# Product 2 of a Strassen-Winograd output by a second level of the method, in the free quarters of the banks of h

## The chip, the cores and the metric

One core of a Trainium2 chip runs the whole kernel. The metric is the time of one execution on the device in microseconds, the median of several runs.

## The reference

Eight heads of a linear attention without softmax, an RMS norm, and then a feed-forward layer with a leaky ReLU, all in fp32:

```python
kv = np.einsum('bhsd,bhse->bhde', k, v)            # batch 8, heads 8, seq 576, dim 64
out = np.einsum('bhsd,bhde->bhse', q, kv)
rms = np.sqrt(np.mean(out * out, axis=-1, keepdims=True) + 1e-06)
attn = out / rms * g_norm
x = attn.transpose(0, 2, 1, 3).reshape(4608, 512)
h = x @ w_in                                       # 512 x 2048
g = np.maximum(0.01 * h, h)
return g @ w_out                                   # 2048 x 512
```

Nearly all the arithmetic is in the two products with w_in and w_out, 4608 x 512 x 2048 each.

## The kernel before, in words

The 4608 tokens are cut into nine blocks of 512. Block 0 is done by plain matmuls (`first_block`). Blocks 1 to 8 (index `i` in the last loop) use the Winograd form of Strassen's method: a product of two matrices cut in 2 x 2 quarters takes seven products of quarters (or of sums of quarters) in place of eight. Its seven products are numbered 1 to 7 and done in the order 1, 2, 6, 5, 7, 3, 4 (`ORDER`). The products 1, 6, 7, 4 pile up in one bank of PSUM and 2, 5, 3 in another, where 2 and 5 start afresh (`FRESH`), so that each partial sum that the method needs stands in a bank at some moment and is taken from there.

The 2048 columns of w_in are cut into four chunks of 512 (`c`). A chunk of a block has two halves: h = x w_in and its leaky ReLU, which gives g (in four quarters g11, g12, g21, g22), and the chunk's share of the output, o, which is g times 512 rows of w_out and is added up over the four chunks in four tiles o11, o12, o21, o22 in SBUF.

h of blocks 2 to 8 (`product_h_two`) uses two levels of the method: 7 x 7 products of 128 x 128 by 128 columns. Step k of the outer seven does seven matmuls of 128 columns: the four with inner numbers 1, 6, 7, 4 go to the bank tagged ha (or hc), side by side in its four quarters of 128 columns, and the three with 2, 5, 3 go to hb (or hd), of which the fourth quarter stays empty. Steps 1, 6, 7 and 4 use ha and hb, steps 2, 5 and 3 use hc and hd. ScalarE copies the banks of steps 1, 6, 5 and 4 into SBUF, VectorE adds those of 2, 7 and 3 to what stands there. After step 4 VectorE forms the four quarters of g from these sums by seven additions, ScalarE applies the leaky ReLU to each, and GpSimd makes the four sums of quarters that the method needs (`sums_of`). g is held in two tiles used in turn by even and odd chunks.

o (`product_o`, one level) takes seven products of four matmuls, 128 rows deep and 256 columns wide, each group of four into one of the two banks oa and oc. Each product's bank is copied (ScalarE, for the first share of a block) or added (VectorE) into one of the four o tiles. The sums of quarters of w_out come from DRAM into two tiles (`pairs`), product by product.

The loop interleaves the two: in each of a chunk's seven slots (`t`) it gives one step of h, then the attention and other small work that lists such as `FINE_SLOTS` place, then one product of o. o runs two slots behind (`LAG`): the first product of a chunk's o stands in slot 2 of the next chunk, the sixth in slot 0 and the seventh in slot 1 of the chunk after. In slot 6 VectorE is also given the first two of the additions for g, and the other five follow the slot's product of o. In slots 20, 21 and 22 of a block (chunk 2 slot 6, chunk 3 slots 0 and 1) VectorE makes the sums of x for the next block, and in slots 24 and 25 and after the block GpSimd makes the second-level sums of x. In the last block the products of o are held back in slots 22 and 25 (`HELD`). Matmuls, DMA and most of VectorE's work are pinned to program order; where an instruction needs a tile that another engine reads or writes, it waits on that engine's semaphore.

The lines of the profile: L118 is the helper that issues every matmul, L610 every addition on VectorE and GpSimd, L781 the leaky ReLU, L845 ScalarE's copies of h's banks, L879 its copies of o's, L646 the loads of the sums of w_out, L708 the loads of w_in's sums. `w_all<-h_ha` and `pairs<-h_hb` are the evictions of h's banks (`qa` and `qc` in the code), and `o<-o_a` those of o's.

Of the kernel before, what the change touches and what calls it, by code (L numbers as in the profile page):

```python
# [9 lines left out]
F32 = mybir.dt.float32  # L10
# [13 lines left out]
def kernel(  # L24
# [584 lines left out]
    def add(eng, out_, a, b_, minus=False, pinned=False):  # L609
        ins = eng.tensor_tensor(out_, a, b_, op=ALU.subtract if minus else ALU.add)  # L610
        if pinned or steady and eng is nc.vector:
            pin(ins)
# [45 lines left out]


    GROUPS = (1, 6, 7, 4), (2, 5, 3)  # L660
    AT = {j: n for n, j in enumerate((5, 6, 7, 3, 1, 2, 4))}
    ORDER = (1, 2, 6, 5, 7, 3, 4)
    FRESH = (1, 2, 5)
# [96 lines left out]

        return sides, quarters, sums(), inner

    def strassen(tags, left, right, done):


        banks = {}
        for i in ORDER:
            b = tags[0 if i in (1, 6, 7, 4) else 1]
            if i in FRESH:
                banks[b] = ps_m.tile([P, 2, N2], F32, tag=b, name=f"{b[0]}_{b[1]}")  # L770
            bank = banks[b]
            for part in range(2):
                for r in range(2):
                    matmul(bank[:, part, :], lhsT=left(i, part, r), rhs=right(i, part, r),
                           start=i in FRESH and part == 0 and r == 0, stop=(r == 1),
                           skip_group_check=True)
            done(i, bank.rearrange("p u (v n) -> p (u v) n", v=2))
            yield
# [45 lines left out]
                            lambda i, part, r: x_sides[i][:, r, :], done)  # L824
        sums_of(c, to)

    def product_h_two(i, c, quarters, to):

        n0 = 7 * ((i - 2) * NC + c)

        into = {1: (0, True), 2: (0, False), 6: (1, True), 5: (3, True), 7: (3, False),
                3: (1, False), 4: (2, True)}
        banks = {}
        for t, k in enumerate(ORDER):
            for js, tags, q in zip(GROUPS, (("ha", "hc"), ("hb", "hd")), (qa, qc)):
                tag = tags[0 if k in (1, 6, 7, 4) else 1]
                if k in FRESH:
                    banks[tag] = ps_m.tile([P, len(js), P], F32, tag=tag, name=f"h_{tag}")
                for n, j in enumerate(js):
                    matmul(banks[tag][:, n, :], lhsT=w_place(n0 + t)[:, AT[j], :],  # L840
                           rhs=quarters[k][j], start=k in FRESH and n == 0, stop=True,
                           skip_group_check=True)
                at, fresh = into[k]
                if fresh:
                    nc.scalar.copy(q[:, at], banks[tag])  # L845
                else:
                    add(nc.vector, q[:, at], banks[tag], q[:, at])
            read(n0 + t + 1 + RING)
            yield
        g11, g21, g22, g12 = g_of(c)  # L850
        add(nc.vector, g21, qa[:, :, 0, :], qa[:, :, 1, :])
        add(nc.vector, g11, qa[:, :, 0, :], qc[:, :, 0, :])
        yield
        add(nc.vector, g22, g21, qa[:, :, 2, :])
        add(nc.vector, g12, g22, qa[:, :, 3, :])
        yield
        add(nc.vector, g22, g22, qc[:, :, 1, :])
# [6 lines left out]
    def product_o(n, g_sides, os, finish):  # L864
# [124 lines left out]
    HELD = (22, 25)  # L989
    o_queue, waited = collections.deque(), 0  # L990

    def go_o():
        while o_queue:
            if next(o_queue[0], o_queue) is not o_queue:
                return True
            o_queue.popleft()

    for i in range(1, NB):
        one = i == 1
        steady = not one  # L1000
        late, a_steps = a_steps, attention(i + 1, fine=not one) if i + 1 < B else iter(())
        os = {}
        for c in range(NC):
            g_sides = {}
            h_steps = product_h(c, h_sides, x_sides, g_sides) if one else \
                product_h_two(i, c, quarters, g_sides)
            for t in range(7):
                slot = 7 * c + t
                go(h_steps, 1)
                if not one:  # L1010

                    if t == 6:
                        go(h_steps, 1)
                    if slot in LATE_SLOTS:
                        go(late, 1)
                    for _ in range(FINE_SLOTS.get(slot, 0)):
                        go(a_steps, 1)
                    if i + 1 < NB:
                        if slot == 20:
                            x_sides, new_quarters, sums, inner = sides_x(i + 1)  # L1020
                        if slot in (20, 21, 22):
                            go(sums, 2 if slot == 20 else 1)
                        if slot == 24:
                            inner(0)
                        elif slot == 25:
                            inner(1)
                    load_some()
                if slot in HELD and i == NB - 1:
                    pass
                elif waited == LAG:  # L1030
                    go_o()
                elif o_queue:
                    waited += 1
                if one:

                    if t == 1:
                        combine(c, 2)
                    if t == 3 and c < NC - 1:
                        h_sides, more_h = sides_w1(c + 1)
                        combine(c + 1, 0)  # L1040
                    if t == 5 and c < NC - 1:
                        more_h()
                        combine(c + 1, 1)
                    if slot == 4:
                        go(late, 1)
                    if slot in A_SLOTS:
                        go(a_steps, 1)
                    load_some()
                    if slot == 24:
                        go(a_steps)  # L1050
                        x_sides, new_quarters, sums, inner = sides_x(i + 1)
                        go(sums)
                    elif slot == 25:
                        inner(0)
# [11 lines left out]
            o_queue.append(product_o((i - 1) * NC + c, g_sides, os, store(i)))  # L1066
    while go_o():
        pass

# [29 lines left out]
```

## Time and profile before

The time is 927.6 us (three runs, 926.85 to 929.41). The profile is of one execution with a span of 925.5 us.

| engine | busy, us | share of the span | instructions |
|---|---|---|---|
| TensorE, matmuls (PE) | 915.1 | 99% | 6856 |
| TensorE, weight loads (PEld) | 776.5 | 84% | 6856 |
| VectorE (DVE) | 615.5 | 67% | 998 |
| ScalarE (ACT) | 328.7 | 36% | 651 |
| GpSimd (POOL) | 317.6 | 34% | 318 |

The engines run side by side, each in its own order, so that the shares don't add up to one. An fp32 matmul stands in the records as two passes with a weight load each. A line of the timeline gives the start in microseconds from the span's start, the duration, the engine, the line of the code, the operation, output and input tiles (buffer numbers left out), sizes and count; at the end, in brackets, how long the engine was idle before it and what released it. Lines that follow each other with the same tiles are merged.

### The profile page before, as it was taken

The page shows a single profiled execution, that of the slowest core. Times are in us where ns is not written, and L with a number is a line of the kernel's source. Part 1 is how long each engine was busy: PE and PEld are TensorE (multiplying, and loading weights), DVE is VectorE, ACT ScalarE, POOL GpSimd, SP SyncE. Part 2 cuts the span into 40 slices and gives each one's busy share as a digit, 9 for nine tenths or more (in the row PEclk, how much of TensorE's full clock was granted, in tenths as well). Part 3 has the DMA queues.
Part 4 walks back from the last instruction along what each step waited for, and adds up shares of the span by engine and source line. Part 5 has one row for each costly group of instructions (what it writes and reads, how often), then busy time and mean ns, then how long its engine had stood idle before and what let it go on. Part 6 is the DMA issues. An engine that isn't in the chain of part 4 may idle for free.

```text
span 925.5 us, 17566 instructions
## 1 busy us (share of the span) xinstructions
PE 915.1 (99%) x6856; PEld 776.5 (84%) x6856; DVE 615.5 (67%) x998; ACT 328.7 (36%) x651; POOL 317.6 (34%) x318
## 2 busy tenths in 40 slices
PE   8999999999999999999999999999999999999998
PEld 5544447888998999899999999999988999999996
DVE  4866995587456876597757875687558744654454
ACT  4544532242135233532343423342333333223330
POOL 2000354967622542236211711272225322532222
PEclk9999999999999999999999999999999999999999
DMA  9999936895598678856995599668755676667632
GB/s 270 223 234 217 238 114 193 276 301 165 150 348 266 185 208 297 274 174 189 280 297 181 173 282 276 219 183 229 252 174 175 197 220 186 185 196 220 187 121 91
DMA packets 90066, 200.03 MB, mean 216 GB/s; under 512 B 9856, under 2 KB 42112, under 8 KB 89984
## 3 DMA queue, kind: packets, MB, share of 16 engines
q1 hardware_dynamic: 79392, 186.85, 68.9%
q10 hardware_dynamic: 10144, 10.88, 3.4%
q8 instruction: 55, 0.90, 0.4%
q0 software_dynamic: 448, 1.18, 0.3%
q14 instruction: 27, 0.22, 0.1%
HBM read 172.39 MB, written 26.48 MB: 215 GB/s over the span
## 4 chain that ended last, share of the span: by engine, by line
PE 95%; DMA 2%; DVE 2%; issue 0%; ACT 0%; POOL 0%; SPq 0%; ACTq 0%; DVEq 0%; POOLq 0%
PE o_a L118 21%; PE o_c L118 21%; PE h_ha L118 11%; PE h_hb L118 8%; PE h_hc L118 8%; PE h_hd L118 6%; PE o_acc L118 6%; PE h_ps L118 6%; PE o_ps L118 2%; PE kv_ps L118 2%; PE h_a L118 1%; PE h_b L118 1%; DMA pairs<-in_v_dram 1%; PE h_c L118 1%; PE h_d L118 1%; DMA pairs<-in_moe_w_in_dram 1%
## 5 line engine op out<-in xcount | busy, mean ns | idle before, releaser
L610 POOL TENSOR_TENSOR gs<-g 128x512 f32<-128x512 f32 x64 | 80.8, 1282 | 442.3 <-ACT g L781 442.3
L610 DVE TENSOR_TENSOR o<-o_c,o 128x512 f32<-128x512 f32 x104 | 71.6, 688 | 117.8 <-PE o_c L118 117.6
L781 ACT ACTIVATE g<-g 128x512 f32<-128x512 f32 x124 | 78.2, 631 | 123.4 <-DVE g L610 123.4
L845 ACT COPY w_all<-h_ha 128x512 f32<-128x512 f32 x84 | 48.7, 580 | 186.6 <-PE h_ha L118 186.6
L610 DVE TENSOR_TENSOR o<-o_a,o 128x512 f32<-128x512 f32 x88 | 60.4, 687 | 63.4 <-PE o_a L118 63.3
L118 PE MATMUL o_c<-pairs,gs 128*128 128x256 f32 x384 | 91.3, 381 | 0.0
L118 PE MATMUL o_a<-pairs,gs 128*128 128x256 f32 x384 | 90.8, 379 | 0.0
L118 PEld LDWEIGHTS o_c<-pairs,gs 128*128 128x128 f32 x384 | 69.8, 190 | 9.3 <-issue 1.4
L118 PEld LDWEIGHTS o_a<-pairs,gs 128*128 128x128 f32 x384 | 69.8, 190 | 7.8
L118 PE MATMUL o_c<-w,g 128*128 128x256 f32 x256 | 61.6, 383 | 0.0
L118 PE MATMUL o_a<-w,g 128*128 128x256 f32 x256 | 61.5, 383 | 0.0
L118 PEld LDWEIGHTS h_ha<-stage,w_all 128*128 128x128 f32 x448 | 58.7, 192 | 2.8
L118 PE MATMUL h_ha<-stage,w_all 128*128 128x128 f32 x448 | 59.0, 275 | 0.0
L118 PE MATMUL h_ps<-xT,w_all 128*128 128x512 f32 (+1 forms) x136 | 57.9, 570 | 0.2 <-DVE w_all L255 0.2
L118 PE MATMUL o_acc<-w,g 128*128 128x512 f32 x128 | 57.8, 595 | 0.0
L610 DVE TENSOR_TENSOR g<-g,pairs 128x512 f32<-128x512 f32 x84 | 55.6, 689 | 1.9
L118 PEld LDWEIGHTS o_a<-w,g 128*128 128x128 f32 x256 | 46.4, 190 | 11.0 <-ACT pairs L845 3.1
L610 POOL TENSOR_TENSOR pairs<-w_all 128x512 f32<-128x512 f32 x8 | 11.5, 1438 | 123.5 <-DMA stage<-in_moe_w_in_dram 95.1
L118 PEld LDWEIGHTS o_c<-w,g 128*128 128x128 f32 x256 | 46.4, 190 | 5.8
L118 PEld LDWEIGHTS h_ps<-xT,w_all 128*128 128x128 f32 x136 | 25.5, 190 | 29.2 <-issue 26.5
L118 PEld LDWEIGHTS o_acc<-w,g 128*128 128x128 f32 x128 | 24.0, 190 | 29.8 <-issue 29.4
L610 DVE TENSOR_TENSOR w_all<-h_hc,w_all 128x512 f32<-128x512 f32 x56 | 38.4, 686 | 15.6 <-PE h_hc L118 15.4
(196 smaller groups left out, 2028.0 us busy)
## 6 DMA issues: line engine op xcount, KB each, us to landing
w_all<-w SPq DMA_DIRECT2D x196, 448.0 KB, 4.3
pairs<-w SPq DMA_DIRECT2D x56, 512.0 KB, 4.5
out_dram<-o ACTq DMA_DIRECT2D x36, 256.0 KB, 4.5
v_in<-in_v_dram SPq DMA_DIRECT2D x29, 288.0 KB, 5.7
k_in<-in_k_dram SPq DMA_DIRECT2D x28, 288.0 KB, 6.3
q_in<-in_q_dram SPq DMA_DIRECT2D x56, 144.0 KB, 6.6
q_in<-in_q_dram SPq DMA_DIRECT2D x56, 140.0 KB, 6.6
w<-stage SPq DMA_DIRECT2D x12, 512.0 KB, 4.6
```

The source lines that it names most:

```text
L118: pin(nc.tensor.matmul(*args, **kw))
L610: ins = eng.tensor_tensor(out_, a, b_, op=ALU.subtract if minus else ALU.add)
L781: nc.scalar.activation(t, t if src is None else src, func=AF.Prelu, alpha=SLOPE)
L845: nc.scalar.copy(q[:, at], banks[tag])
```

## The change

For 28 chunks (from the third of block 1 to the second of block 8), product 2 of o, which is g12 times the lower left quarter of w_out's chunk, is no longer done as four matmuls of 256 columns in o's own order. It is done by a second level of the method: seven products of 128 x 128 by 128 columns. Each of the seven has its place in the step of h with the same number, two chunks later, and goes into the empty fourth quarter of hb or hd, whose pattern of fresh starts and piling up is the one that it needs. VectorE adds that quarter into one quarter of o11 after each step (`Second.done`).

For it GpSimd makes four differences and sums of g12's quarters in each chunk (`inner_g`, into free room of `pairs`), and once for each of the four chunks of w_out those of its quarter (`inner_w2`, over a part of w_out that is no longer used). o's order becomes 1, 5, 6, 3, 7, nothing, 4, the slot of "nothing" being slot 0 of a chunk; the tiles of o are taken in another order, since o11 is now finished last; and the load of the first pair of w_out's sums follows product 6. The purpose is fewer columns on TensorE: seven matmuls of 128 columns in place of four of 256.

```diff
+    INTO = {1: (0, 0), 2: (0, 0), 6: (0, 1), 3: (0, 1), 7: (1, 1), 5: (1, 1), 4: (1, 0)}
...
-    def strassen(tags, left, right, done):
+    def strassen(tags, left, right, done, order=ORDER):
...
-        for i in ORDER:
+        for i in order:
+
+            if i is None:
+                yield
+                continue
...
+    gi = view(pairs, 12 * P, 4, P)
...
+    def inner_g(c, half):
+
+        g = g_of(c)[3]
+        a11, a21, a12, a22 = (g[:, n, :] for n in range(4))
+        s1, s2, s3, s4 = (gi[:, n, :] for n in range(4))
+        if half == 0:
+            add(nc.gpsimd, s1, a21, a22)
+            add(nc.gpsimd, s2, s1, a11, True)
+        else:
+            add(nc.gpsimd, s3, a11, a21, True)
+            add(nc.gpsimd, s4, a12, s2, True)
+
+    class Second:
...
+        def product(self, k, bank):
+            matmul(bank, lhsT=self.left[k], rhs=self.right[k], start=False, stop=True,
+                   skip_group_check=True)
+
+        def done(self, k, bank):
+            v, s = INTO[k]
+            to = self.o[:, v, s * P:s * P + P]
+            add(nc.vector, to, bank, to)
+            if self.n % NC == NC - 1 and k == ORDER[-1]:
+                self.finish("11", self.o)
+
-    def product_h_two(i, c, quarters, to):
+    def product_h_two(i, c, quarters, to, second):
...
-                    banks[tag] = ps_m.tile([P, len(js), P], F32, tag=tag, name=f"h_{tag}")
+                    banks[tag] = ps_m.tile([P, 4, P], F32, tag=tag, name=f"h_{tag}")
                 for n, j in enumerate(js):
                     matmul(banks[tag][:, n, :], lhsT=w_place(n0 + t)[:, AT[j], :],
                            rhs=quarters[k][j], start=k in FRESH and n == 0, stop=True,
                            skip_group_check=True)
+                if len(js) < 4 and second:
+                    second.product(k, banks[tag][:, 3, :])
                 at, fresh = into[k]
+                bank = banks[tag][:, :len(js), :]
                 if fresh:
-                    nc.scalar.copy(q[:, at], banks[tag])
+                    nc.scalar.copy(q[:, at], bank)
                 else:
-                    add(nc.vector, q[:, at], banks[tag], q[:, at])
+                    add(nc.vector, q[:, at], bank, q[:, at])
+                if len(js) < 4 and second:
+                    second.done(k, banks[tag][:, 3, :])
...
-            for key in ("11", "12", "21", "22"):
+
+            for key in ("12", "22", "11", "21"):
...
-            if i == 5:
+            if i == (6 if second else 5):
                 sums(0)
...
-                            lambda i, part, r: w_sides[i][:, r, :], done)
+                            lambda i, part, r: w_sides[i][:, r, :], done,
+                           (1, 5, 6, 3, 7, None, 4) if second else ORDER)
...
+                now = (i - 1) * NC + c
+                if now >= NC - 1 and now - 1 in seconds:
+                    for half in range(2):
+                        if t == (6 if one or half else 4):
+                            inner_g((now - 1) % NC, half)
+                    if t == 5 and now <= 2 * NC - 2:
+                        inner_w2((now - 1) % NC)
...
+            by_two = NC - 2 <= n < NC * (NB - 1) - 2
+            if by_two:
+                seconds[n] = (os, store(i))
```

More of the change, by code (lines that the diff above doesn't have):

```diff
@@ L825, in product_h, with inner_w2, __init__ @@
         sums_of(c, to)
-    def product_h_two(i, c, quarters, to):
+    gi = view(pairs, 12 * P, 4, P)
+    def inner_w2(c):
+        y = w2_sb[1][c]
+        t1, t2, t3, t4 = (w2_sb[0][c][:, u, N2 + s * P:N2 + s * P + P]
+                          for u in range(2) for s in range(2))
+        y11, y12, y21, y22 = (y[:, u, s * P:s * P + P] for u in range(2) for s in range(2))
+        add(nc.gpsimd, t1, y12, y11, True)
+        add(nc.gpsimd, t2, y22, t1, True)
+        add(nc.gpsimd, t3, y22, y12, True)
+        add(nc.gpsimd, t4, y21, t2, True)
+    def inner_g(c, half):
[9 more added lines that the diff above has]
+    class Second:
+        def __init__(self, n, o, finish):
+            self.n, self.o, self.finish = n, o, finish
+            c = n % NC
+            g, y = g_of(c)[3], w2_sb[1][c]
+            ts = [w2_sb[0][c][:, u, N2 + s * P:N2 + s * P + P]
+                  for u in range(2) for s in range(2)]
+            self.left = {1: g[:, 0, :], 2: g[:, 2, :], 4: g[:, 3, :],
+                         **{k: gi[:, at, :] for at, k in enumerate((5, 6, 7, 3))}}
+            self.right = {1: y[:, 0, :P], 2: y[:, 1, :P], 3: y[:, 1, P:N2],
+                          **{k: ts[at] for at, k in enumerate((5, 6, 7, 4))}}
+        def product(self, k, bank):
[8 more added lines that the diff above has]
+    def product_h_two(i, c, quarters, to, second):
         n0 = 7 * ((i - 2) * NC + c)
@@ L862, in product_h_two, with product_o @@
         sums_of(c, to)
-    def product_o(n, g_sides, os, finish):
+    def product_o(n, g_sides, os, finish, second):
         c = n % NC
@@ L990, with second_of @@
     o_queue, waited = collections.deque(), 0
+    seconds = {}
+    def second_of(n):
+        if n in seconds:
+            os_, finish = seconds.pop(n)
+            return Second(n, os_["11"], finish)
     def go_o():
@@ L1005 @@
             h_steps = product_h(c, h_sides, x_sides, g_sides) if one else \
-                product_h_two(i, c, quarters, g_sides)
+                product_h_two(i, c, quarters, g_sides, second_of((i - 1) * NC + c - 2))
             for t in range(7):
@@ L1065 @@
                 read((2, 4, RING, RING)[c])
-            o_queue.append(product_o((i - 1) * NC + c, g_sides, os, store(i)))
+            n = (i - 1) * NC + c
+            by_two = NC - 2 <= n < NC * (NB - 1) - 2
+            if by_two:
+                seconds[n] = (os, store(i))
+            o_queue.append(product_o(n, g_sides, os, store(i), by_two))
     while go_o():
```

## The prediction

> **What bounds the kernel now.** I read the share of busy time and the chain of waits first, then the groups by shape, then the timeline around one place: the seam between two chunks of h.
>
> ```profile
> PE 915.1 (99%) x6856; PEld 776.5 (84%) x6856; DVE 615.5 (67%) x998; ACT 328.7 (36%) x651; POOL 317.6 (34%) x318
> PE 95%; DMA 2%; DVE 2%; issue 0%; ACT 0%; POOL 0%; SPq 0%; ACTq 0%; DVEq 0%; POOLq 0%
> ```
>
> TensorE is the bound, and the chain that ends last runs through it for 95% of the span. So a microsecond less of TensorE is a microsecond less of time, as long as nobody makes TensorE wait. What it waits for are banks of PSUM, and who empties them, and when, is seen in the timeline. This is the seam of two chunks in a stretch with little else to do (lines chosen; start, duration, engine, instruction):
>
> ```profile
> 475.37 1.89 PE L118 MATMUL o_a<-pairs,gs 128*128 128x256 f32 x8
> 475.57 0.48 ACT L845 COPY pairs<-h_hb 128x384 f32<-128x384 f32 x1
> 475.57 0.69 DVE L610 TENSOR_TENSOR g<-w_all 128x512 f32<-128x512 f32 x1 [2.16 <-ACT w_all L845]
> ...
> 477.10 0.38 PE L118 MATMUL h_ha<-xT,w_all 128*128 128x128 f32 x2
> ...
> 477.30 0.69 DVE L610 TENSOR_TENSOR o<-o_a,o 128x512 f32<-128x512 f32 x1 [0.43 <-PE o_a L118]
> ...
> 479.42 2.02 DVE L610 TENSOR_TENSOR g<-g,pairs 128x512 f32<-128x512 f32 x3
> ...
> 480.39 0.38 PE L118 MATMUL h_hc<-xT,w_all 128*128 128x128 f32 x2
> ...
> 481.47 0.63 ACT L781 ACTIVATE g<-g 128x512 f32<-128x512 f32 x1 [0.42 <-DVE g L610]
> 481.95 1.89 PE L118 MATMUL o_a<-pairs,g 128*128 128x256 f32 x8
> 482.01 0.46 ACT L845 COPY pairs<-h_hb 128x384 f32<-128x384 f32 x1
> ...
> 483.68 0.50 PE L118 MATMUL h_ha<-stage,w_all 128*128 128x128 f32 x3
> ```
>
> Call 475.37, where step 4 of a chunk's h has ended, zero. TensorE then does o (to 1.73), h step 1 (to 3.29), o, h step 2, o, and h step 6 at 8.31: a product of o is always 1.73 us and a step of h 1.56, without a gap. Beside it runs a chain: VectorE makes the four g of the chunk that ended (7 adds) with o's evictions between them, ScalarE applies the leaky ReLU to each, and only behind the last ReLU does ScalarE copy the hb bank of step 1 out, 6.64 to 7.10. Step 6 writes that bank from 8.31 + 0.89 = 9.20 on. The slack is 2.1 us.
>
> The same copy in a seam where VectorE also makes sums of x (zero is 499.40), in a seam at a block's end where GpSimd is busy (zero is 523.43), and in the last seam (zero is 880.51), where one product of o is held back:
>
> ```profile
> 500.83 0.69 DVE L610 TENSOR_TENSOR w_all<-xT 128x512 f32<-128x512 f32 x1
> ...
> 506.87 0.46 ACT L845 COPY pairs<-h_hb 128x384 f32<-128x384 f32 x1
> ```
>
> ```profile
> 523.63 1.11 DVE L610 TENSOR_TENSOR g<-w_all 128x512 f32<-128x512 f32 x1 [0.87 <-ACT w_all L845]
> ...
> 530.23 0.46 ACT L845 COPY pairs<-h_hb 128x384 f32<-128x384 f32 x1
> ```
>
> ```profile
> 887.09 1.06 PE L118 MATMUL h_ha<-stage,w_all 128*128 128x128 f32 x8
> 887.14 0.46 ACT L845 COPY pairs<-h_hb 128x384 f32<-128x384 f32 x1
> ```
>
> It ends at 7.93, 7.26 and 7.09. In the last seam step 6 stands at 6.58 and needs hb at 7.47: slack 0.4.
>
> [...] The trace shows each fp32 matmul as two passes with two loads, starting every 111 ns at 128 columns and every 213 ns at 256; a quarter-size matmul therefore can't go much under 0.22 us. [...]
>
> ```profile
> L610 DVE TENSOR_TENSOR w_all<-h_hc,w_all 128x512 f32<-128x512 f32 x56 | 38.4, 686 | 15.6 <-PE h_hc L118 15.4
> L610 DVE TENSOR_TENSOR pairs<-h_hd,pairs 128x384 f32<-128x384 f32 x56 | 31.0, 553 | 0.0
> ```
>
> [...] the first add at the block's end takes 1.11 us against 0.69.
>
> **The change part by part.**
>
> *TensorE.* 28 chunks lose product 2 of o (4 matmuls, 1.73 us) and gain 7 matmuls of 128 columns. From the timeline, 8 passes of h_ha take 0.89, so two take 0.2225, and seven matmuls 1.56. Gain 0.17 a chunk, 28 x 0.17 = 4.8 us. This is all there is to win: 922.8.
>
> *Added work elsewhere.* GpSimd: 4 subtractions of 128x128 a chunk (a 128x128 one there takes 0.45 to 0.68 us in the groups by shape, so 1.8 to 2.7 us, on an engine 34% busy; their last wait is for step 3, so they are done by the seam). VectorE: seven adds of 128x128[...], for one of 0.69: 1.3 us a chunk, 37 us in all at 67% busy, hidden inside a chunk because h and o banks there come round after 5 to 6 us. The table of w2 for it is made once on GpSimd, and "11" of a block is stored two chunks later, both beside other work: nothing. The loads of the w2 sums are asked for at least three slots ahead of their use, some 10 us, and land in 4.5 us (the DMA issues): nothing.
>
> *The wait at the seam.* Here the change does three things at once. First, o's slot at step 1 is empty (the None in the order): TensorE goes from step 1 straight to step 2, and step 6 comes 1.73 us earlier, less twice 0.22 for the quarters in steps 1 and 2: hb is written at 9.20 - 1.73 + 0.44 = 7.91, its first weight load at 7.80. Second, each fresh bank hb now has two readers, ScalarE for three quarters and VectorE for the fourth[...]. In the built order VectorE's add for step 4 stands ahead of the adds for g, and its add for step 1 behind them. Third, step 6's first matmul into hb waits for that last add. Queued behind it on TensorE is everything.
>
> Quiet seam: the copy of step 4 ends at 0.68; VectorE's quarter 0.78 to 1.07 (0.1 for a hand-over between engines, as between the copy and the add at 475.57); g starts at 0.98 instead of 0.20, the second add 1.59, o's eviction 2.20 instead of 1.93 (it used to wait 0.43 for TensorE, which takes up part of the delay). From that eviction to the end of the copy of step 1 it is 7.10 - 1.93 = 5.17, so the copy ends at 7.37, the quarter at 7.76, TensorE may go at 7.8. It wants 7.80. A tie: 0 to 0.15, I take 0.05, for 14 seams 0.7 us.
>
> Seam with sums of x (one in each of six blocks): two more adds fill the gap, so the whole delay of 0.76 comes through: 7.93 + 0.76 = 8.69, quarter to 9.08, go at 9.1: wait 1.3, 6 x 1.3 = 7.8 us.
>
> Seam at a block's end (six): 7.26 + 0.5 to 0.78 (part is won back because the adds then miss some of GpSimd's work): go at 8.15 to 8.45, wait 0.35 to 0.65, I take 0.5: 3.0 us.
>
> Last seam: go at about 7.8 as in the quiet one; hb is wanted at 6.58 - 1.73 + 0.44 + 0.89 - 0.11 = 6.07: 1.7 us.
>
> Sum: 0.7 + 7.8 + 3.0 + 1.7 = 13.2 of waits, less 4.8: +8.4, **936.0 us**. Bounds: with 0 in quiet seams, 1.2 and 0.35 in the others and 1.5 in the last 10.8, so 933.6; with 0.15, 1.5, 0.8 and 1.9 17.8, so 940.6.
>
> **The rivals.** *A: no wait.* Only the 4.8 us count: 922.8. For it: TensorE has no gap anywhere in the steady part, and the skipped eviction frees VectorE at 5.99 (the o add after the adds for g). Against: that add comes after the chain, and takes nothing off it. *B: waits at the busy seams alone, and shorter* (VectorE's and ScalarE's hand-overs cost less than I put, some 0.4 us at each): 6 x 0.9 + 1.3 + 6 x 0.1 = 7.3, less 4.8: 930.1. *C: VectorE becomes the bound in stretches.* In halves of a block with attention it is busy about 80% (40.3 of the 50 us from 600 to 650, in the table of stretches), the fresh steps' quarters make it wait for ScalarE, and the backlog reaches the quiet seams: another 0.6 us in each of 14: 944.4. Against: one to two microseconds a chunk leave it below 90%.
>
> **How the numbers follow.** Forecast 0.62, A 0.12, B 0.13, C 0.13. B lies at the edge of "same" and gives it half. Faster 0.12, same 0.07, slower 0.81. The range holds the forecast with its bounds, B, and most of C, and leaves out A and the worst of C: 927 to 944.
>
> **What would show it.** Right: weight loads of h_hb at step 6 waiting for VectorE's add into o, 1 us and more once in each block, near none in quiet seams; matmuls of h_hb and h_hd into the fourth quarter at 0.22 us; VectorE's busy time up by some 35 us. Wrong: no such wait (A), waits at steps 7, 3 or 4 or at o's banks (C), or the first weight load of hb going ahead of the quarter's add.

## The result and the profile after

The changed kernel takes 940.15 us (median of four runs, 938.09 to 942.89) against 928.5 (four runs, 926.85 to 929.84) of the kernel before on the same chip. The ratio is 1.0128, with a 95% interval of 1.0096 to 1.0161: slower, and close to the 936.0 of the forecast, on the high side of it. On the base of 927.6 us, to which the ratios below are also brought, it is 939.5.

Engines and the chain of work that ended last, from the page of the kernel after (span 938.6 us):

```profile
PE 917.5 (98%) x7024; PEld 780.2 (83%) x7024; DVE 642.8 (68%) x1166; ACT 329.0 (35%) x651; POOL 374.1 (40%) x446
PE 80%; DVE 11%; ACT 3%; POOL 2%; issue 1%; DMA 1%; SPq 0%; ACTq 0%; DVEq 0%
```

TensorE's busy time didn't fall (917.5 us against 915.1), though its columns did: the ends of matmuls are modelled in these records, and a part of a short wait is counted as busy (in the seam below, eight passes of h_ha from 513.17 stand for 1.05 us, where the starts of eight take 0.89). The second line is the one to read. The chain that sets the end ran through TensorE for 95% of the span; now 14% of it is VectorE's and ScalarE's. They have not become the bound by their sums (68% and 35% busy), but in short stretches TensorE stands behind them.

The groups by shape (busy us and mean ns of one, then the idle time before them and what ended it):

```profile
L610 DVE TENSOR_TENSOR o<-h_hb,o 128x128 f32<-128x128 f32 x112 | 32.2, 287 | 83.9 <-ACT pairs L906 83.9
L118 PE MATMUL h_hb<-stage,w_all 128*128 128x128 f32 x336 | 48.0, 279 | 9.2 <-DVE o L610 9.2
L610 POOL TENSOR_TENSOR pairs<-g 128x128 f32<-128x128 f32 x56 | 25.5, 455 | 77.3 <-PE h_hb L118 62.9
L610 DVE TENSOR_TENSOR o<-h_hd,o 128x128 f32<-128x128 f32 x84 | 23.9, 284 | 39.5 <-ACT pairs L906 38.9
```

The first line holds both halves of the forecast mechanism. The new quarter add costs 287 ns, and the idle time before it was ended by ScalarE's copy of the other three quarters, all 83.9 us of it. The two engines take turns at the bank in this trace: in the seam shown below the add starts 0.03 us after the copy has ended. The second line is the price on TensorE: 9.2 us before matmuls of h_hb, ended by that add. The weight loads tell the same story in the list of waits, 8 times and at most 1.3 us: six seams with sums of x, the last seam, and one at the entry to block 2.

```profile
PEld h_hb L118 <- DVE o L610: 9.2, 8, 1.3
```

A seam with sums of x in the timeline (lines chosen); step 4 has ended, and zero is, at 506.14:

```profile
506.39 0.48 ACT L906 COPY pairs<-h_hb 128x384 f32<-128x384 f32 x1 [0.31 <-PE h_hb L118]
506.90 0.29 DVE L610 TENSOR_TENSOR o<-h_hb,o 128x128 f32<-128x128 f32 x1 [1.65 <-ACT pairs L906]
507.11 0.68 DVE L610 TENSOR_TENSOR g<-w_all 128x512 f32<-128x512 f32 x1
...
513.17 1.05 PE L118 MATMUL h_ha<-stage,w_all 128*128 128x128 f32 x8
513.80 0.63 ACT L787 ACTIVATE g<-g 128x512 f32<-128x512 f32 x1 [0.42 <-DVE g L610]
514.34 0.46 ACT L906 COPY pairs<-h_hb 128x384 f32<-128x384 f32 x1
514.83 0.29 DVE L610 TENSOR_TENSOR o<-h_hb,o 128x128 f32<-128x128 f32 x1 [1.06 <-ACT pairs L906]
515.18 0.94 PE L118 MATMUL h_hb<-stage,w_all 128*128 128x128 f32 x6 [0.95 <-DVE o L610]
```

VectorE's quarter of step 4 runs from 0.76 to 1.05, and g starts at 0.97 where it started at about 0.2. The copy of hb ends 8.66 after zero, the quarter at 8.98, TensorE restarts at 9.04. The prediction had 8.69, 9.08 and 9.1.

Where the 11 us went. From the starts of the matmuls I took, for each product of o and each step of h, what it lasted beyond its 1.73 and 1.56 us, in both traces. From the first step of block 2's h to the end, the kernel before takes 925.51 - 231.36 = 694.15 us and the kernel after 938.64 - 233.41 = 705.23, which is 11.1 more:

| where | predicted, us | in the trace, us |
|---|---|---|
| fewer columns | -4.8 | -4.8 (8 passes of h_hb take 0.89, two 0.2225) |
| six seams with sums of x | 6 x 1.3 = 7.8 | 6 x 1.22 = 7.3 |
| six seams at a block's end | 6 x 0.5 = 3.0 | 6 x 0.50 = 3.0 |
| last seam | 1.7 | 1.6 |
| fourteen quiet seams | 0.7 | 0.2 |
| entry to block 2 | 0 | 2.8 |
| banks of o, at 321, 811 and in the last block | 0 | 0.7 |
| sum | +8.4 | +10.8 |

A wait's number includes some 0.1 us by which the next matmul came late after TensorE had stood still (an example is at 259.24 below: two passes in 0.49 us in place of 0.38 to 0.39); 0.3 of the 11.1 us are not placed. The rest of the difference between the two profiled spans, 2 us, lies ahead of block 2, where the changed parts don't run (the first matmul of block 0's output stands at 36.15 against 34.11). In this profile and in two others (sums of x later, without the add of step 1) the granted clock of TensorE was 0.5 for 3.4 us from about 19 us on, and these three start latest, at 36.1 to 36.2; all the others lie between 33.5 and 35.1, kernels with the same beginning among them. So these 2 us are of the execution and not of the kernel.

The entry is the part that the prediction doesn't have. In the timeline of the kernel after, lines chosen: GpSimd (POOL), SyncE's queue (SPq), ScalarE's queue (ACTq), ScalarE and TensorE.

```profile
240.33 0.46 POOL L610 TENSOR_TENSOR pairs<-pairs,g 128x128 f32<-128x128 f32 x1
...
241.42 0.46 POOL L610 TENSOR_TENSOR pairs<-g,pairs 128x128 f32<-128x128 f32 x1
...
248.22 0.87 POOL L610 TENSOR_TENSOR w<-w 128x128 f32<-128x128 f32 x2
...
249.05 0.99 POOL L610 TENSOR_TENSOR w<-w,w 128x128 f32<-128x128 f32 x2
...
249.99 1.27 POOL L610 TENSOR_TENSOR pairs<-w,pairs 128x512 f32<-128x512 f32 x1
...
251.29 0.32 SPq L654 DMA_DIRECT2D w<-pairs  x1
...
252.18 2.15 SPq L159 DMA_DIRECT2D q_in<-in_q_dram  x4
...
258.17 0.39 ACTq L970 DMA_DIRECT2D out_dram<-o  x1
258.60 0.59 ACT L906 COPY w_all<-h_ha 128x512 f32<-128x512 f32 x1 [11.80 <-PE o_c L118]
259.24 0.49 PE L118 MATMUL h_ha<-xT,w_all 128*128 128x128 f32 x2 [0.73 <-ACT w_all L906]
```

The same sum of w_out in the kernel before:

```profile
245.33 1.29 POOL L610 TENSOR_TENSOR pairs<-w,pairs 128x512 f32<-128x512 f32 x1
```

Read from the bottom. The step 4 whose bank ha ScalarE copies at 258.60 began at 254.83, so the bank was full by about 256; ScalarE came late because its own store of o12 stood ahead, and TensorE paid 0.9 us here and 1.0 more at the next step 6. In the trace ScalarE's wait ahead of this store ends at 258.12, 0.03 us after the third of the four loads of q from 252.18 on has landed (at 258.09), and in the built program the store waits for the semaphore that an earlier load of q raises. These loads were asked for shortly behind the store of w_out's sums, which waited for GpSimd's last sum of w_out (249.99 to 251.26). GpSimd had no idle time to speak of from 230.3 to 252.6 (busy for 8.00 of the 8 us from 232 to 240, for 7.92 of those from 240 to 248); its new sums for the second level (the first four lines, 2.8 us in all) stand in that row of work. Counted from the first step of block 2's h, that last sum of w_out starts at 16.6 us; in the kernel before at 14.0 (245.33 - 231.36). A third wait, of 0.7 us near 240, is TensorE's own for GpSimd's first sums of g12.

### The profile page after: what moved, and what is told of

It is laid out like the page before. It is cut to its first block, busy times and chain, and to the rows that moved or that the text cites. A ratio compares the mean times of both kernels' runs of the same rounds, so it can differ in the third digit from the quotient of the medians.

```text
span 938.6 us, 18186 instructions
## 1 busy us (share of the span) xinstructions
PE 917.5 (98%) x7024; PEld 780.2 (83%) x7024; DVE 642.8 (68%) x1166; ACT 329.0 (35%) x651; POOL 374.1 (40%) x446
## 4 chain that ended last, share of the span: by engine, by line
PE 80%; DVE 11%; ACT 3%; POOL 2%; issue 1%; DMA 1%; SPq 0%; ACTq 0%; DVEq 0%
PE o_c L118 15%; PE o_a L118 15%; PE h_hb L118 9%; DVE g L610 8%; PE h_ha L118 8%; PE h_hd L118 6%; PE h_hc L118 6%; PE o_acc L118 6%; PE h_ps L118 6%; PE o_ps L118 2%; PE kv_ps L118 2%; DVE o L610 2%; PE h_a L118 1%; POOL stage L610 1%; ACT pairs L906 1%
## 5 line engine op out<-in xcount | busy, mean ns | idle before, releaser
L610 POOL TENSOR_TENSOR gs<-g 128x512 f32<-128x512 f32 x64 | 83.2, 1320 | 274.7 <-ACT g L787 272.6
L610 DVE TENSOR_TENSOR o<-h_hb,o 128x128 f32<-128x128 f32 x112 | 32.2, 287 | 83.9 <-ACT pairs L906 83.9
L610 DVE TENSOR_TENSOR o<-o_c,o 128x512 f32<-128x512 f32 x90 | 61.8, 686 | 32.7 <-PE o_c L118 27.3
L610 DVE TENSOR_TENSOR o<-o_a,o 128x512 f32<-128x512 f32 x74 | 50.7, 685 | 34.3 <-PE o_a L118 34.0
L118 PE MATMUL h_hb<-stage,w_all 128*128 128x128 f32 x336 | 48.0, 279 | 9.2 <-DVE o L610 9.2
L610 POOL TENSOR_TENSOR pairs<-g 128x128 f32<-128x128 f32 x56 | 25.5, 455 | 77.3 <-PE h_hb L118 62.9
L118 PEld LDWEIGHTS h_hb<-stage,w_all 128*128 128x128 f32 x336 | 41.9, 192 | 11.8 <-DVE o L610 9.2
L610 DVE TENSOR_TENSOR o<-h_hd,o 128x128 f32<-128x128 f32 x84 | 23.9, 284 | 39.5 <-ACT pairs L906 38.9
L906 ACT COPY pairs<-h_hb 128x384 f32<-128x384 f32 x84 | 39.8, 474 | 25.8 <-PE h_hb L118 25.4
```

The lines of the kernel that those rows point to most:

```text
L118: pin(nc.tensor.matmul(*args, **kw))
L906: nc.scalar.copy(q[:, at], bank)
```

## The experiments

Ratios are against the kernel before; us are those ratios times 927.6, so that runs of different chips can be read side by side.

| kernel | ratio, 95% interval | us | extra in a seam with sums of x |
|---|---|---|---|
| changed kernel | 1.0128, 1.0096 to 1.0161 | 939.5 | 1.22 |
| empty slot after product 5 (gap_mid) | 0.9974, 0.9964 to 0.9983 | 925.2 | 0 |
| empty slot after product 6 (gap_5) | 0.9987, 0.9974 to 0.9999 | 926.4 | 0 |
| new order of o alone | 1.0008, 0.9996 to 1.0019 | 928.3 | 0 |
| empty slot, no second level | 0.9544, 0.9528 to 0.9559 | 885.3 | 0.6 |
| without the adds of steps 1 and 4 | 0.9993, 0.9983 to 1.0002 | 926.9 | 0.15 |
| without the add of step 1 | 1.0064, 1.005 to 1.0078 | 933.5 | 0.9 |
| without the add of step 4 | 1.0026, 1.0016 to 1.0037 | 930.0 | 0.45 |
| last ReLUs after step 1 | 1.0059, 1.0038 to 1.0079 | 933.1 | 0.75 |
| sums of x two slots later | 1.0113, 1.0095 to 1.013 | 938.1 | 0.1 |
| store of o12 by SyncE | 1.0103, 1.0087 to 1.012 | 937.2 | 1.22 |
| entry's new sums by VectorE | 1.0152, 1.013 to 1.0174 | 941.7 | 1.22 |
| the same, empty slot after product 5 | 1.0021, 1.0008 to 1.0034 | 929.5 | 0 |

**Move the empty slot.** The theory: TensorE waits because the empty slot at step 1 brings step 6 1.73 us closer, while the chain that empties hb got longer. The rival: the two readers of the bank cost this anywhere. The empty slot goes from slot 0 of the later chunk to slot 4 of the earlier one, so that products 3 and 4 of o stand between the steps of a seam again:

```diff
-                           (1, 5, 6, 3, 7, None, 4) if second else ORDER)
+                           (1, 5, None, 6, 7, 3, 4) if second else ORDER)
```

> The changed kernel with o's order 1, 5, nothing, 6, 7, 3, 4: the empty slot moves from slot 0 to slot 4 of a chunk, away from the seam; all else stays. Theory (the empty slot at the seam brings step 6 forward by 1.73 us, before VectorE's add of step 1): step 6 wants hb at 9.5 again while the add is done at 7.8 to 9.1, so the waits of 1.2, 0.5 and 1.6 us at the seams go, the gain of 4.8 on TensorE stays, and some 2 us of waits at the entry from block 1 may stay: 925, 0.3 to 0.5% under the kernel before. Rival (the seven added VectorE operations and the second reader cost wherever they stand): 936 to 940.

It takes 0.9974 of the time before, the fastest of the versions that compute all of the output and faster than both kernels. The same copy and add in a seam with sums of x (step 6 begins at 506.77):

```profile
506.21 0.46 ACT L906 COPY pairs<-h_hb 128x384 f32<-128x384 f32 x1
506.70 0.29 DVE L610 TENSOR_TENSOR o<-h_hb,o 128x128 f32<-128x128 f32 x1 [1.06 <-ACT pairs L906]
506.77 1.05 PE L118 MATMUL h_ha<-stage,w_all 128*128 128x128 f32 x8
507.56 0.75 PEld L118 LDWEIGHTS h_hb<-stage,w_all 128*128 128x128 f32 x6
```

The chain is the same to the hundredth (the quarter again starts 1.06 us after VectorE's last work), but the weight load of hb comes 0.57 us after the quarter has ended, and has no wait. So the second reader costs nothing where a product of o covers it. Of the 4.8 us won, some 2.0 are still given back: 0.8 at the entry, 0.2 at the end, and two waits for a bank of o, of which this is the larger:

```profile
304.36 1.99 PE L118 MATMUL o_c<-pairs,gs 128*128 128x256 f32 x8 [0.39 <-DVE o L610]
```

Here product 7 follows product 6 into the same bank in the very next slot. That makes -2.8, and the ratio says -2.4.

The other place for the empty slot, between product 6 and product 7:

```diff
-                           (1, 5, 6, 3, 7, None, 4) if second else ORDER)
+                           (1, 5, 6, None, 7, 3, 4) if second else ORDER)
```

> The changed kernel with o's order 1, 5, 6, nothing, 7, 3, 4: the empty slot at slot 5. With the empty slot at slot 4 products 6 and 7 stood in neighbouring slots and in the same bank, and 7 waited 0.4 to 0.6 us for VectorE in the blocks without attention beside it; here a step and a slot lie between. Theory: those waits go, the seams stay free of waits (hb wanted at 9.5, add done by 9.1 to 9.5 in seams with sums): within 1 us of the run with the gap at slot 4 or up to 1 us less, 0.3 to 0.4% under the kernel before. Rival (VectorE is late at the seam, since step 3 and step 4 now follow each other and step 3's evictions lie right ahead of step 4's add): 2 to 4 us more.

The seams are free here too, and what is left is 0.3 at each of two banks of o and 1.7 at the entry. Its interval and that of the version above overlap (0.9974 to 0.9999 and 0.9964 to 0.9983), so it is no better.

**The order without the rest.** The kernel before with the new order of o, the new order of its tiles and the later load of w_out's sums, product 2 done in full in the slot that the change leaves empty:

```diff
-        for i in ORDER:
+        for i in order:
...
-            for key in ("11", "12", "21", "22"):
+            for key in ("12", "22", "11", "21"):
...
-            if i == 5:
+            if i == (6 if by_two else 5):
...
-                            lambda i, part, r: w_sides[i][:, r, :], done)
+                            lambda i, part, r: w_sides[i][:, r, :], done,
+                           (1, 5, 6, 3, 7, 2, 4) if by_two else ORDER)
```

> The kernel before with the changed kernel's order of o for the same 28 chunks, product 2 itself standing in the slot that is empty there (1, 5, 6, 3, 7, 2, 4), the o tiles in the changed order and the first load of w_out's sums after product 6. No second level. Theory: order, tiles and load cost nothing: 927 to 929, like the kernel before. Rival (part of the loss is o's banks, tiles or loads in the new order): 931 or more, with waits of weight loads of oa and oc.

1.0008, no measurable difference, and no new wait in its trace. Order, tiles and load cost nothing by themselves.

**The empty slot without the second level.** The same order with None for product 2. Product 2 of those 28 chunks is left out altogether, so the time shows what the empty slot does, and without any wait it would be 927.6 - 28 x 1.73 = 879.2. Of its edit against the kernel before, the line that leaves the slot empty:

```diff
-                            lambda i, part, r: w_sides[i][:, r, :], done)
+                            lambda i, part, r: w_sides[i][:, r, :], done,
+                           (1, 5, 6, 3, 7, None, 4) if by_two else ORDER)
```

> The kernel before in the changed order with the empty slot at the seam (1, 5, 6, 3, 7, nothing, 4) and product 2 left out of 28 chunks altogether, with no second level: every hb bank has one reader, ScalarE. It saves 28 x 1.73 = 48.4 us on TensorE: 879.2 without waits. Theory (the empty slot alone already makes a wait where g's chain is long): step 6 wants hb at 9.20 - 1.73 - 0.11 = 7.36, the copy ends at 7.93 in six seams with sums (wait 0.65), at 7.1 to 7.3 elsewhere (none), and 1.5 in the last seam: 884 to 885. Rival (no wait without the second reader): 879 to 880.

It gives 885.3, 6 us above that. No quarter is read by VectorE here, and still TensorE stands, now behind ScalarE's copy:

```profile
PEld h_hb L118 <- ACT pairs L848: 4.5, 7, 1.0
```

Seven times: 0.5 us (once 0.85) at each seam with sums of x, and 1.06 plus 0.35 in the last. Another 1.6 us lie at the entry to block 2, where TensorE waits for loads of w_in's sums. So the empty slot alone uses up the slack where g's chain is long. Step 6 comes 0.45 us earlier here than in the changed kernel, since steps 1 and 2 have no quarter products (2 x 0.2225); with these, but without the two adds, 0.15 us of the 0.6 is left in a seam with sums, as the next experiment shows.

**The two quarter adds at a seam.** Three kernels leave out VectorE's add of the fourth quarter into o11 after step 1, after step 4, or after both; the product on TensorE stays, only that share of o11 is never added.

```diff
-            add(nc.vector, to, bank, to)
+            if k not in (1, 4):
+                add(nc.vector, to, bank, to)
```

> The changed kernel without VectorE's adds of the quarters of steps 1 and 4 (so product 2's shares of these two steps are left out of the output); the matmuls and the empty slot stay. Theory (the wait needs both causes): the hb bank of step 1 has one reader again and g is no longer delayed by step 4's quarter, so the copy ends at 7.9 in seams with sums and at 7.1 to 7.3 in the others, against 7.8 wanted: waits of 0.2 in six seams, 1.1 in the last, none at block ends: 930 to 932. Rival (the empty slot alone): 938 to 940. Rival (the second reader alone, the slot doesn't matter): 925.

> The changed kernel without VectorE's add of the quarter of step 1 alone (its share of product 2 is left out of the output). Theory (two delays add up: step 4's add holds g back by 0.76 us, step 1's comes 0.3 to 0.4 us behind ScalarE's copy): the copy still ends at 8.66 in seams with sums, go at 8.75 against 7.8 wanted: 0.95 in six seams, 0.1 at block ends, 1.35 in the last: 934 to 936. Rival (the second reader of step 1's own bank is all of it): 928 to 930, as without both adds.

> The changed kernel without VectorE's add of the quarter of step 4 alone (its share of product 2 is left out of the output). Theory: g is no longer held back, the copy of step 1 ends at 7.9 in seams with sums, VectorE's add at 8.3, go at 8.4 against 7.8: 0.6 in six seams, none at block ends, 1.45 in the last: 932 to 933. Rival (step 4's add is all of it): 928 to 930. With the run without step 1's add, the two savings should come to 11 or 12 us together.

Without both, 926.9, some 3 us under the 930 to 932 expected, though the waits themselves are near those of the expectation: 0.15 a seam with sums, 0.96 in the last, and the entry. By the number alone the rival of the second reader alone (925) is as near; it fails on the kernel with the empty slot after product 5, where the second reader stays and costs nothing. Without step 1's add alone, 933.5, in the expected range, and TensorE's weight loads wait for ScalarE's copy in place of VectorE:

```profile
PEld h_hb L118 <- ACT pairs L907: 6.5, 8, 1.0
```

Without step 4's add alone, 930.0, below the 932 to 933 expected and at the edge of what the rival said (step 4's add is all of it: 928 to 930). What speaks against the rival are the loads, which still wait for VectorE's add of step 1, 4.5 us in all:

```profile
PEld h_hb L118 <- DVE o L610: 4.5, 8, 1.3
```

So of the 1.22 us in a seam with sums, step 4's add (0.7 us at the head of g's chain, since everything on VectorE is queued behind its wait for ScalarE) brings about 0.75, and step 1's, at the tail, about 0.35. The two savings, 5.9 and 9.5 us by the ratios, add up to 15.4, not to the 11 or 12 expected nor to the 12.5 of both together. In the traces, from the first step of block 2's h to the end, they are 4.6 and 7.2 against 11.4, which does fit; the ratio of the changed kernel, which enters the sum of the savings twice, is known to some 3 us only.

**Shorten the chain another way.** If the chain is what counts, work taken out of it elsewhere must help too. The leaky ReLU of g22 and g21 and GpSimd's sums of g are given out after step 1 of the next chunk, behind ScalarE's copy of hb:

```diff
-        for t in (g11, g12, g22, g21):
-            relu(t)
-        sums_of(c, to)
+        relu(g11)
+        relu(g12)
+
+        def rest():
+            relu(g22)
+            relu(g21)
+            sums_of(c, to)
...
+            pending.append(rest)
```

> The changed kernel, but in each seam the leaky ReLU of g22 and g21 and GpSimd's sums of g are given out after step 1 of the next chunk's h, so that ScalarE's copy of step 1's hb stands ahead of the last ReLU. Theory (the whole chain of g's additions, ReLUs, copy of hb and VectorE's quarter is what TensorE waits for): the copy still can't run before VectorE's last three additions have read the old copy, so that only the last ReLU's part of the chain falls away, some 0.4 us a seam: the seams with sums of x wait 0.8 in place of 1.2 us, the block ends 0 to 0.1 in place of 0.5, the last seam 1.2 in place of 1.6; 934 to 936 us, unless the later ReLUs delay a product of o that reads g22 or g21. Rival (the wait is one between ScalarE and VectorE on the bank alone, 0.3 to 0.4 us): no change, 940.

933.1: the theory's direction and size, a little better than it said. The copy of hb ends at 8.19 in place of 8.66, and the waits fall to 0.65, to 0 to 0.24 at the block ends, and to 0.92 in the last seam. The rival, which put the wait down to the bank alone, falls: the bank's readers are unchanged here.

**Take the sums of x out of those seams.** They go from slots 20 and 21 to slots 22 and 23:

```diff
-                        if slot == 20:
+                        if slot == 22:
...
-                        if slot in (20, 21, 22):
-                            go(sums, 2 if slot == 20 else 1)
+                        if slot in (22, 23):
+                            go(sums, 3 if slot == 22 else 1)
```

> The changed kernel with VectorE's sums of x moved from slots 20, 21 and 22 to slots 22 (three) and 23 (one), behind the seam between chunks 2 and 3. Theory (in those six seams the two sums fill the gap that swallows the delay elsewhere): their waits of 1.2 us go to near 0 as in quiet seams, 6 x 1.2 = 7.2 us less; o's first banks may wait up to 0.5 us instead: 933 to 936. Rival (the sums' place doesn't matter, the wait is 1 us in every such seam for other work of that part of the block): 938 to 940.

The seams' waits fell to 0.1 at most, as the theory said, but the time is 938.1, not the 933 to 936 expected. The saving came back two slots on, in the timeline of this kernel:

```profile
419.40 1.75 DVE L610 TENSOR_TENSOR xT<-xT 128x512 f32<-128x512 f32 x1
...
421.08 0.68 DVE L610 TENSOR_TENSOR o<-o_c,o 128x512 f32<-128x512 f32 x1
...
421.86 1.97 PE L118 MATMUL o_c<-pairs,gs 128*128 128x256 f32 x8 [0.77 <-issue]
```

VectorE's sums of x now stand ahead of its eviction of product 4 from oc, which ends at 421.76, and product 5 starts 0.1 us after it. The releaser is given as "issue", that is, the profile names none; the eviction is the one reader of that bank, and the next start follows it. Such waits of 0.6 to 1.9 us in six blocks sum to 6.9 us. So VectorE has room for these sums in neither of the two places that were tried.

**The store at the entry.** o12 of block 1 is stored by SyncE, so that ScalarE has nothing to wait for:

```diff
-            nc.scalar.dma_start(
+            (nc.sync if i == 1 and key == "12" else nc.scalar).dma_start(
```

> The changed kernel, but the store of o12 of block 1 is issued by SyncE in place of ScalarE; nothing else. Theory (at the entry to block 2 ScalarE stood still behind this store, which waited for an earlier load of q, and so copied ha of step 4 two microseconds late): TensorE's waits of 1.0 and 1.1 us between 258 and 266 us go, the one of 0.7 us for GpSimd near 240 stays; some 2 us less, 938. Rival (ScalarE was late for another cause, VectorE's or GpSimd's work at the entry): the copy of ha comes as late as before and the time stays at 940.

ScalarE's part of the theory holds: neither wait of TensorE behind the late copy of ha is there any more. But two others have come, 0.3 and 1.3 us, so that the waits of the entry come to 2.3 us in place of 2.6 (the 2.8 of the table counts the late starts after them too). The larger, with the load that it is for:

```profile
263.70 2.47 SPq L710 DMA_DIRECT2D w_all<-w  x3
...
267.06 1.13 PE L118 MATMUL h_hc<-stage,w_all 128*128 128x128 f32 x8 [1.14 <-DMA w_all<-w]
```

Counted from the first step of block 2's h, this load is asked for at 32.1 us, in the changed kernel at 31.9 (265.34 - 233.41). So it comes when it came before, and TensorE, freed of the earlier waits, is only there earlier to wait for it. In both kernels the DMA engines are busy all the time from 256 to 272: none of the 40 slices of 255 to 272 has them under 80%, and they move 357 GB/s in the mean. The ratio's interval overlaps that of the changed kernel: no gain is shown, and taking away the store's wait alone is not enough.

**The entry's new sums off GpSimd.** In the last chunk of block 1 and the first of block 2, VectorE makes the second-level sums of g12 and of w_out:

```diff
-    def inner_w2(c):
+    def inner_w2(c, eng):
...
-        add(nc.gpsimd, t1, y12, y11, True)
+        add(eng, t1, y12, y11, True)
...
+                eng = nc.vector if now <= NC else nc.gpsimd
                 if now >= NC - 1 and now - 1 in seconds:
```

and likewise `inner_g`; once in the changed kernel, and once with the empty slot after product 5.

> The changed kernel, but in the last chunk of block 1 and the first of block 2 the second-level sums of g12 and of w_out are made by VectorE, which is about half busy there, in place of GpSimd, which has no idle time there from 230 to 253 us. Theory (the entry's loss begins on GpSimd: its sums for the second level push w_out's sums back by 2.6 us against the first step of block 2; SyncE stands behind the store of these sums, asks for q 2.6 us later, and ScalarE's store of o12 waits for q): the waits of 0.7, 0.9 and 1.0 us at the entry go, q is asked for some 2 us earlier, 2 to 3 us less in all, a ratio near 1.010; the seams stay as they are. Rival (the DMA engines are full there, and the q loads land late however early they are asked for): the wait of 0.7 goes, the others stay, a ratio near 1.012.

> The order with the empty slot after product 5 (slot 4), and the entry's second-level sums by VectorE as in the kernel beside it. Theory: the seams stay free, the 0.8 us at the entry go as well; the time before less 4.8 plus 1.2, some 924 us, a ratio of 0.996 to 0.997. Rival (the entry is not GpSimd's doing): 0.9974 as without it.

From the first step of block 2's h on, both do what the theory said. No wait of TensorE is left at the entry; q is asked for 11.4 us after that step and not 18.8; the way from there to the end is 702.4 us against 705.2, and with the slot after product 5 692.6 against 693.3 (theory: 2 to 3 less, and 0.8 less). So the entry's loss does begin on GpSimd. But both are slower as wholes, and my expectation of the time failed. Earlier, in block 1, the new place of these sums makes a wait that I had not looked for (the second of the two kernels):

```profile
214.69 1.53 DVE L610 TENSOR_TENSOR w<-w 128x128 f32<-128x128 f32 x2 [6.69 <-POOL pairs L610]
...
219.94 3.66 PE L118 MATMUL o_a<-w,g 128*128 128x256 f32 x8 [4.04 <-DVE o L610]
```

The first sum of w_out overwrites a part of w_out that GpSimd's other sums still read. On GpSimd's own queue that costs nothing (in the changed kernel it stood idle for 0.2 us in all ahead of the eight such sums); VectorE stands 6.7 us for it, its evictions of o stand behind, and TensorE stands 4.0, in both kernels. A second loss followed that stop. After it the passes of 256 columns start every 0.427 us for a while and not every 0.216, with a granted clock of 0.55 (second kernel, from 219.90 to 223.70 us), which costs another 1.8 us. From the first matmul of block 1's h to the first step of block 2's, the first kernel takes 93.7 us against 87.7 and the second 91.9 against 85.9: 6.0 more in each. Less what is won at the entry that makes 3.2 us for the first and 5.3 for the second, where the ratios went up by 0.24% and 0.47%, or 2.2 and 4.4 us; the difference is within the intervals. Moving only g12's sums, or that sum later, should leave this stop out; it was not run.

## Why the prediction was right

**What bounds it, and what can be won.** Right. The quarter products cost 0.2225 us each, the gain is 4.8 us, and with the waits gone it is the part that remains. One reading was a little off and entered no sum: a pass of 256 columns starts every 216 ns (1.73 us for eight), not every 213.

**The second reader.** Right. VectorE's quarter waits for ScalarE's copy at each fresh step; it starts 0.03 us after the copy has ended, and not the 0.1 that I allowed for the hand-over. Ahead of the result that wait was my assumption: in the kernel before every bank had one reader, so no trace showed what two do.

**The seams.** Right in kind and in size: 1.22 against 1.3, 0.50 against 0.5, 1.6 against 1.7, and the quiet ones, forecast as a tie, are one (hb's copy ends 7.34 after zero, forecast 7.37). Two causes were summed there, the empty slot and the two adds, and it takes both: the adds make no wait where the empty slot stands elsewhere (gap_mid), and the empty slot with the quarter products but without the two adds makes 0.15 of the 1.22 (0.6 where the quarter products are left out too). At a block's end a part of the delay was won back, as forecast, but only some 0.1 us: beside GpSimd's sums of x VectorE's first two adds for g took 1.11 and 0.94 us in the kernel before (from 523.63) and 1.26 and 0.68 in the changed one (from 532.15; those sums end at 532.86), where GpSimd stood still 0.69 and 0.69 (from 475.57).

**What was too low.** The sum was 8.4 and the trace has 10.8. The step that was off is the "nothing" for the table of w2, the stores and GpSimd's sums, "beside other work" and "done by the seam". It holds in the steady part and fails once, at the entry from block 1 to block 2, at 2.8 us: there GpSimd has no idle time, and what it does late, SyncE's loads and ScalarE's store do late in turn. I had costed the steady chunk and taken the first one to be like it. That GpSimd starts it is shown by the last two kernels; that the store waited for q is read from the built program and from the landing in the trace. Smaller, 0.7 us, are the waits at banks of o, where "hidden inside a chunk" did not hold at three places. Together 3.5 us stood at nothing, and the waits at the seams were put 1.1 us too high; that these two partly cancel, so that 2.4 are left, is luck.

**The other work.** VectorE's 196 quarter adds take 56.1 us, the 28 skipped evictions were 19.5, together +36.6 as forecast. A quarter add took 287 ns in hb and 284 in hd; an estimate from the two adds out of PSUM in the trace before (686 ns at 512 columns, 553 at 384, so 1.04 ns a column) gives 287. The busy time rose by 27.3 alone, since it counts overlaps once: an add that follows another starts some 0.08 us before the other's record ends. GpSimd's 128x128 adds for g12's sums took 0.455 us, the lower end of what I gave. VectorE did not become the bound (rival C): no wait at quiet seams. A fell on the seams' waits. B had the same places with 0.9 and 0.1, near to what the kernel without step 1's add shows (0.9 in a seam with sums), but the hand-overs that it doubted are a small part of the delay (0.03 us from copy to add, 0.06 from add to TensorE): most is the wait for the copy itself.

## What to carry to other kernels

Work put into a free corner of a buffer was paid for here by the buffer's release (9.2 us before matmuls of h_hb), not by its arithmetic (0.2225 us a product, 287 ns an add): ask who empties it now, behind what that engine's instruction is queued, and when the next writer comes. A slot that a change leaves empty is slack that moves from one wait to another, so it belongs where the chain to the next writer is short; here the same work with the slot in another place went from 1.3% slower to 0.26% faster. And cost the first and the last pass as well as the steady one, since loads, stores and set-up meet there.

## What the runs showed of the hardware beyond that

- A wait cost TensorE more than its length: after each stop of 0.4 to 1.4 us the next matmuls came about 0.1 us late on top (for example, the first two passes took 0.49 and not 0.38 to 0.39 at 259.24).
- After a stop of 4.0 us TensorE ran at half its rate for some 3.4 us: passes of 256 columns started every 0.427 us in place of 0.216 (both kernels with the entry's sums on VectorE). The longest stops in the steady part of the other kernels, 1.5 to 1.8 us, were not followed by this. One of 2.04 us in block 0 was (the first of these two kernels, a mean clock of 0.94 from 90 to 120 us), and among stops of 1.7 to 2.4 us near 18 us it followed in three profiles (the changed kernel, 2.1 us: clock 0.5 for 3.4 us) and did not in six (the kernel before, 1.7 us: clock 1.00 up to 24 us), so the runs show no length from which on it happens.
- Where two engines read one bank in turn, the second started 0.03 us after the first had ended (changed kernel: copy's end 514.80, add's start 514.83; 506.87 and 506.90).
- An instruction that waited held up what was queued behind it on its engine: ScalarE stood some 2 us behind a store, SyncE 11.9 us behind a store of sums that weren't made yet, VectorE 6.7 us behind an addition.
- GpSimd's adds of 128x512 elements for the sums of g took 1.29 to 1.35 us in the mean in the changed kernel, its 128x128 ones for the sums of g12 0.455. By an estimate from 1.32 and 0.455, some 0.17 us of the latter are fixed (0.865 us for 384 columns more, 0.288 for 128).
